# Second product of a two-layer token kernel: tasks of 256 columns with a shared fourth lane, another order of the work in the first steps and of the last stores

## The chip, the cores and the metric

The kernel runs on one core of one Trainium2 chip. The metric is the device time of one execution in microseconds, the median of ten runs. A core has a matrix engine (PE, with its weight loads shown apart as PEld), a vector engine (DVE), an activation engine (ACT), GpSimd (POOL), and a queue engine (SP) that here only issues transfers.

## The reference

`x` is 8 x 4096 x 192. Each of 8 heads (24 channels each) is convolved causally along the sequence with 7 taps, whose weights are a softmax of `weight`. The result, 32768 tokens of 192 channels, goes through two dense layers with a sigmoid gate between:

```python
w = np.exp(w); w = w / (np.sum(w, axis=-1, keepdims=True) + 1e-09)
out = np.einsum('hk,bskhg->bshg', w, x_unf)       # x_unf: 7 shifted copies of x
...
h = x @ w_in                                      # 192 -> 2048
g = h * (1.0 / (1.0 + np.exp(-1.702 * h)))
return (g @ w_out).astype(np.float32)             # 2048 -> 192
```

All of it is in 32-bit floats.

## The kernel before

**Steps.** The batch is split in two halves (n = 0, 1). A step takes 256 tokens of each half; there are 64 steps (`N_ST`), and two steps share one convolved chunk of 512 tokens (a "big"). A step has a first product (`w_in`), the gate, and a second product (`w_out`).

**Seven products instead of eight.** Both layers are seen as 2 x 2 block matrices times 2 x 2 block matrices (weights split by output half m and inner half, tokens by half n), and are multiplied with seven block products in a Strassen-Winograd scheme; step 0 alone uses the plain eight. For the second layer the seven are P1 = A11 B11, P2 = A12 B21, P3 = S4 B22, P4 = A22 T4, P5 = S1 T1, P6 = S2 T2, P7 = S3 T3. A and S are blocks of `w_out` and sums of them, B the gated activations, T sums of those (`sum_g`, on the vector engine).

**First product.** It is done in two units a and b of a step (half of the hidden channels each). `product1` issues four matmuls for each call, two on the upper and two on the lower 64 rows of the array, 256 columns each. A unit has the calls `p1`, `p2` (two), `p3` (two), `p4` (two), `p5`, `p5b`, `p6`, `p7`: eleven calls. Results go to PSUM tiles: three `slot` tiles that rotate (unit number modulo 3 gives `x`, the one before gives `z`), and one tile `sums`, which ACT fills with the first product of the unit (`seed`, a copy) and reads out twice (`keep2`, `keep3`). The vector engine adds `z` to the kept sums (`add22`, `add12`), ACT applies the gate (`h11`, `h21`, `h22`, `h12`).

**Second product.** `product2` gives one of the seven products: 96 output channels (three chunks of 32) by 256 tokens, summed over eight blocks j of 128 hidden channels. The array is used in four column lanes of 32. The table `LANES` cuts the 3 x 256 columns into four lanes of 192, so that for each j six matmuls are issued: lane 0 has 192 columns, lane 1 has 64 and 128, lane 2 has 128 and 64, lane 3 has 192. `output` issues P1, P3, P2 (added onto P1 in PSUM), P6, P7, P5, P4 into two banks each of the slots `ra` and `rb`, combines them on 128 partitions x 192 columns, transposes (`turn`), and `store` writes them out with 12 transfers on SP.

**What is hidden under PE.** The convolution of the next chunk runs on the vector engine. `prepare(big)` is a list of 31 pieces: 3 transposes of x, the load of the chunk after, a new buffer, 21 taps, 4 differences (`sums_c`) and `cross`, two transfers that copy the result to the other 64 partitions. `work(n)` runs the next n pieces at the place in the program where it stands. Each engine executes in the order of the program text; nothing reorders it (`manual_schedule`), and the waits between engines follow from the tiles that are read and written, a whole PSUM tile (both banks) at a time: a write of a slot waits for earlier reads of that slot.

**Names and lines of the profile:** L390 first-product matmul, L486 second-product matmul, L413 gate, L423 `seed`, L430 `keep2`, L443 `keep3`, L460 `add22`, L470 `add12`, L479 `sum_g`, L351/L353 taps, L360 `sums_c`, L336 transposes of x, L366 `cross`, L504 `turn`, L510/L514 copies of P1 and P3, L520 to L531 the combination, L543 stores, L665 the transposes of step 0.

Of the kernel before, what the change touches and what calls it, by code (L numbers as in the profile page):

```python
# [8 lines left out]
F32 = mybir.dt.float32  # L9
# [6 lines left out]
def kernel(  # L16
# [27 lines left out]
    nc = tc.nc  # L44
# [5 lines left out]
    P = 128  # L50
    R = 64
    Q = 32
    NC = D // R
    HF = F // 2
    HD = D // 2
    T = 256
    TA = 3 * T // 4
    TOK = 2 * T
    NF = F // P
    NK = NF // 2  # L60
# [11 lines left out]


    LANES = [
        (0, 0, 0, TA, 0),
        (1, 0, TA, T - TA, 0),
        (2, 1, T // 2, T // 2, 0),
        (3, 2, T - TA, TA, 0),
        (1, 1, 0, T // 2, T - TA),
        (2, 2, 0, T - TA, T // 2),  # L80
    ]
# [399 lines left out]
    def product2(slot, bank, a, b, first=True):  # L481
        dst = slot[:, bank, 0:TA]
        for j in range(NK):

            for l, c, t, n, at in LANES:
                nc.tensor.matmul(  # L486
                    dst[l * Q : (l + 1) * Q, at : at + n],
                    w_out_s[:, a, j, c * Q : (c + 1) * Q],
                    g[:, b, j, t : t + n],
                    start=(first and j == 0 and at == 0),  # L490
                    stop=(j == NK - 1),
                    skip_group_check=True,
                )
        return dst

    def output(s, last, work):

        ra, rb = last.x, last.z
        ut = u_pool.tile([P, 4, TA], F32, name="u")
        osb = osb_pool.tile([P, 2, TA // Q, 2 * Q], F32, name="osb")  # L500
        u1, u2, u3, u7 = (ut[:, i, :] for i in range(4))

        def turn(m, n, src):
            vec.transpose(  # L504
                osb[:, n, :, m * Q : (m + 1) * Q],
                src.rearrange("p (j t) -> p j t", t=Q),
            )

        p1 = product2(ra, 0, A11, B11)
        act.copy(u1, p1)  # L510
        for i in range(4):
            last.sum_g(i)
        p3 = product2(rb, 0, S4, B22)
        act.copy(u7, p3)  # L514
        work(2 if s > 1 else None)
        c11 = product2(ra, 0, A12, B21, first=False)
        turn(0, 0, c11)
        work(2)
        p6 = product2(rb, 1, S2, T2)
        vec.tensor_add(u2, u1, p6)  # L520
        work(3)
        p7 = product2(ra, 1, S3, T3)
        p5 = product2(ra, 0, S1, T1)
        vec.tensor_add(u3, u2, p7)  # L524
        vec.tensor_add(u1, u3, p5)
        vec.tensor_add(u2, u2, p5)
        turn(1, 1, u1)
        vec.tensor_add(u2, u2, u7)
        turn(0, 1, u2)
        p4 = product2(rb, 0, A22, T4)  # L530
        vec.tensor_sub(u3, u3, p4)  # L531
        turn(1, 0, u3)

        store(s, osb)

    def store(s, osb):
        big, odd = divmod(s, 2)
        p, c = divmod(big, CHUNKS)
        t = c * TOK + odd * T
        for n in (1, 0):  # L540
            rows = out_v[n, p, t : t + T, :].rearrange("(j i) (c e) -> c i j e", i=Q, e=2 * Q)
            for l, c, t0, nt, at in LANES:
                nc.sync.dma_start(  # L543
                    out=rows[c, :, t0 // Q : (t0 + nt) // Q, :],
                    in_=osb[l * Q : (l + 1) * Q, n, at // Q : (at + nt) // Q, :],
                )
# [3 lines left out]
    def work(n=None):  # L550
        for _ in range(len(todo) if n is None else min(n, len(todo))):
            todo.pop(0)()
# [22 lines left out]
    def first_step():  # L575
# [73 lines left out]
        osb = osb_pool.tile([P, 2, TA // Q, 2 * Q], F32, name="osb")  # L649
        for k in range(2):  # L650
            for n in range(2):
                for m in range(2):
                    src = product2(
                        slots[1 - n],
                        m,
                        (A11, A12, A21, A22)[2 * m + k],
                        (B11, B12, B21, B22)[2 * k + n],
                        first=(k == 0),
                    )
                    if k == 1:  # L660
                        if n == m == 0:
                            work(5)
                            sums_w_out()
                        work(1)
                        vec.transpose(  # L665
                            osb[:, n, :, m * Q : (m + 1) * Q],
                            src.rearrange("p (j t) -> p j t", t=Q),
                        )
        store(0, osb)
# [3 lines left out]
    for s in range(1, N_ST):  # L673
        a, b = nxt or Unit(s, 0), Unit(s, 1)
        if nxt is None:
            a.p1()
            a.seed()
            a.p5()
            a.p5b()
            a.p6()  # L680
        else:
            a.p6()
            a.p5()
            a.p5b()
        nxt = Unit(s + 1, 0) if s + 1 < N_ST and s != 1 else None
        a.keep2()
        a.p7()
        a.keep3()
        a.p2()
        a.h11()  # L690
        work(6)
# [4 lines left out]
        b.p1()  # L696
        b.seed()
        a.p3()
        work(None if s % 2 and s > 1 else 4)
# [12 lines left out]
        work(2)  # L712
# [13 lines left out]
        output(s, b, work)  # L726
        if s % 2 and (s + 3) // 2 < N_BIG:
            todo += prepare((s + 3) // 2)

# [29 lines left out]
```

## Time and profile before

| | us |
|---|---|
| median of 10 runs | 2478.3 (2476.86 to 2479.18) |
| the profiled execution, its own time | 2477.03 |
| its span, first to last instruction | 2475.2 |
| PE busy in the span | 2450.6 (99%) |
| vector engine busy | 1701.2 (69%) |
| ACT busy | 941.2 (38%) |
| mean granted TensorE clock | 0.997 |

The page gives for each engine its busy time, and for each source line the number of instructions, their busy time together, the mean of one and the idle time of the engine ahead of them. A matrix multiplication of 32-bit floats is executed as two passes, so the counts of matmuls in the profile are twice those of the program. Matmuls overlap each other, so a mean duration of one is not the time that it adds. From step 3 on the steps repeat: in the chain of waits the second product of a step takes 18.61 us and is followed by the next step's first product.

### The profile page before, as it was taken

The numbers are of one execution on the slowest core, as the hardware profiler recorded it, in microseconds if no ns is written. First come the engines' busy times: TensorE is split into PE (matmuls) and PEld (weight loads), VectorE is DVE, ScalarE is ACT, GpSimd is POOL, SyncE is SP. The second block draws the span as 40 slices with busy tenths as digits, with TensorE's granted clock in tenths as the row PEclk, the third lists the DMA queues.
The fourth block names the chain that finished last, engine by engine and source line by source line (L and its number), as shares of the span: only waits on it lengthen the run. The fifth ranks groups of instructions, "written<-read, shape, count | busy, mean of one in ns | idle before, by whom it ended". The sixth has DMA issues, their size and how long they took to land.

```text
span 2475.2 us, 114515 instructions
## 1 busy us (share of the span) xinstructions
PE 2450.6 (99%) x54434; PEld 2283.7 (92%) x54434; DVE 1701.2 (69%) x2348; ACT 941.2 (38%) x1052; POOL 8.1 (0%) x27
## 2 busy tenths in 40 slices
PE   8899999999999999999999999999999999999998
PEld 6899999999999999999999999999999999999998
DVE  8576666776666766667766667666677666676654
ACT  5243343343433433433434334334333343343342
POOL 1000000000000000000000000000000000000000
PEclk9999999999999999999999999999999999999999
DMA  7222221221221222212212212222122122122110
GB/s 180 46 55 47 45 58 39 48 57 38 55 59 30 57 47 45 58 38 47 58 38 54 59 29 57 47 45 57 41 46 58 38 54 59 29 58 44 24 35 16
DMA packets 197732, 123.58 MB, mean 50 GB/s; under 512 B 116048, under 2 KB 191440, under 8 KB 193296
## 3 DMA queue, kind: packets, MB, share of 16 engines
q1 hardware_dynamic: 196960, 115.48, 22.1%
q8 instruction: 425, 6.96, 1.2%
q0 software_dynamic: 288, 0.79, 0.1%
q14 instruction: 43, 0.35, 0.1%
q10 hardware_dynamic: 16, 0.00, 0.0%
HBM read 53.15 MB, written 25.17 MB: 32 GB/s over the span
## 4 chain that ended last, share of the span: by engine, by line
PE 97%; DVE 2%; DMA 0%; ACT 0%; issue 0%; SPq 0%; DVEq 0%; ACTq 0%
PE slot L486 48%; PE slot L390 31%; PE sums L390 18%; DVE g L479 0%; DVE f L353 0%; DMA f<-f 0%; DMA xin<-in_x_dram 0%; DVE xt L336 0%; ACT u L430 0%; ACT g L413 0%; SPq L114 0%; DVE u L460 0%; DVE f L360 0%; DVE w_out_s L249 0%; DVE f L244 0%
## 5 line engine op out<-in xcount | busy, mean ns | idle before, releaser
L486 PEld LDWEIGHTS slot<-g,w_out_s 128*32 128x32 f32 x43104 | 1192.2, 110 | 32.0 <-issue 24.0
L486 PE MATMUL slot<-g,w_out_s 128*32 128x128 f32 (+2 forms) x43104 | 1204.7, 274 | 9.1 <-DVE osb L665 5.0
L390 PE MATMUL slot<-f,w_in_s 64*128 64x256 f32 x7200 | 843.7, 376 | 0.6 <-DMA f<-f 0.5
L390 PEld LDWEIGHTS slot<-f,w_in_s 64*128 64x128 f32 x7200 | 693.0, 187 | 88.1 <-DVE u L460 1.4
L479 DVE TENSOR_TENSOR g<-g 128x1024 f32<-128x1024 f32 x504 | 600.1, 1222 | 192.4 <-ACT g L413 188.1
L390 PE MATMUL sums<-f,w_in_s 64*128 64x256 f32 x4080 | 512.0, 379 | 2.8 <-ACT u L430 2.3
L430 ACT COPY u<-sums 128x1024 f32<-128x1024 f32 x126 | 127.5, 1012 | 996.6 <-PE sums L390 996.6
L390 PEld LDWEIGHTS sums<-f,w_in_s 64*128 64x128 f32 x4080 | 390.6, 187 | 52.6 <-ACT u L430 3.1
L353 DVE SCALAR_TENSOR_TENSOR f<-xt,cw,f 128x512 f32<-128x512 f32 x564 | 421.8, 748 | 14.4
L413 ACT ACTIVATE g<-u 128x1024 f32<-128x1024 f32 x252 | 265.6, 1054 | 14.2 <-DVE u L470 14.1
L470 DVE TENSOR_TENSOR u<-u,slot 128x1024 f32<-128x1024 f32 x126 | 153.4, 1218 | 68.5 <-PE slot L390 68.5
L460 DVE TENSOR_TENSOR u<-u,slot 128x1024 f32<-128x1024 f32 x126 | 153.2, 1216 | 55.7 <-ACT u L443 55.7
L524 DVE TENSOR_TENSOR u<-u,slot 128x192 f32<-128x192 f32 x63 | 22.4, 355 | 244.5 <-PE slot L486 244.5
L443 ACT COPY u<-sums 128x1024 f32<-128x1024 f32 x126 | 127.5, 1012 | 130.8 <-PE sums L390 130.8
L413 ACT ACTIVATE g<-sums 128x1024 f32<-128x1024 f32 x128 | 130.5, 1019 | 94.7 <-PE sums L390 94.7
L413 ACT ACTIVATE g<-slot 128x1024 f32<-128x1024 f32 x132 | 135.5, 1027 | 50.1 <-PE slot L390 50.1
L423 ACT COPY sums<-slot 128x1024 f32<-128x1024 f32 x126 | 126.8, 1006 | 48.0 <-PE slot L390 46.0
L520 DVE TENSOR_TENSOR u<-u,slot 128x192 f32<-128x192 f32 x63 | 22.3, 354 | 92.0 <-PE slot L486 92.0
L514 ACT COPY u<-slot 128x192 f32<-128x192 f32 x63 | 20.1, 319 | 144.8 <-PE slot L486 144.8
L504 DVE STREAM_TRANSPOSE osb<-u 128x192 f32<-128x192 f32 x189 | 71.0, 376 | 4.3
L336 DVE STREAM_TRANSPOSE xt<-xin 128x576 f32<-128x576 f32 x96 | 67.1, 750 | 1.6 <-DMA xin<-in_x_dram 1.5
L360 DVE TENSOR_TENSOR f<-f 128x256 f32<-128x256 f32 x128 | 51.3, 422 | 2.2
(78 smaller groups left out, 287.5 us busy)
## 6 DMA issues: line engine op xcount, KB each, us to landing
xin<-in_x_dram SPq DMA_DIRECT2D x240, 180.0 KB, 4.3
f<-f SPq DMA_DIRECT2D x62, 576.0 KB, 4.8
out_dram<-osb SPq DMA_DIRECT2D x256, 48.0 KB, 1.7
out_dram<-osb SPq DMA_DIRECT2D x256, 32.0 KB, 1.6
out_dram<-osb SPq DMA_DIRECT2D x256, 16.0 KB, 1.5
g<-in_moe_w_in_dram SPq DMA_DIRECT2D x8, 384.0 KB, 9.3
g<-in_moe_w_out_dram SPq DMA_DIRECT2D x4, 768.0 KB, 5.5
xin<-in_x_dram SPq DMA_DIRECT2D x16, 160.0 KB, 3.1
```

Source lines behind the costliest of these rows:

```text
L336: vec.transpose(xts[big][:, c, :, :].rearrange("p n (j t) -> p (n j) t", t=Q), xins[big].rearrange("p n j d -> p (n j) d")[:, :, c * R : c ...
L353: vec.scalar_tensor_tensor(out=dst, in0=src, scalar=tap, in1=dst, op0=ALU.mult, op1=ALU.add)
L390: nc.tensor.matmul(slot[:, h, j * T : (j + 1) * T], w_in_s[halves[h], u, a, j * P : (j + 1) * P], f[halves[h], 0 if h == o else 1, b, :], ...
L413: act.activation(g[:, b, j : j + NK // NU, :].rearrange("p f t -> p (f t)"), src.rearrange("p h n -> p (h n)"), AF.Gelu_apprx_sigmoid,)
L423: act.copy(sums, self.x)
L430: act.copy(self.u2, sums)
L443: act.copy(self.u3, sums)
L460: vec.tensor_add(self.u3, self.u3, self.z)
L470: vec.tensor_add(self.u2, self.u2, self.z)
L479: vec.tensor_sub(v[dst], v[a], v[b])
L486: nc.tensor.matmul(dst[l * Q : (l + 1) * Q, at : at + n], w_out_s[:, a, j, c * Q : (c + 1) * Q], g[:, b, j, t : t + n], start=(first and j ...
L504: vec.transpose(osb[:, n, :, m * Q : (m + 1) * Q], src.rearrange("p (j t) -> p j t", t=Q),)
```

## The change

The second product is cut differently. A task (`product2`) now has 256 columns in each of the four lanes: lanes 0 to 2 are the three chunks of one product, and lane 3 is one chunk of P3 or P4. Five tasks carry P1, P2, P6, P5 and P7 in lanes 0 to 2; their fourth lanes carry the three chunks of P3 (with P1, P2, P6) and two of P4 (with P5, P7). The last chunk of P4 is made by `quarters`: each lane sums two of the eight j blocks, and the four quarters are added afterwards. P2 gets a place of its own in PSUM and is added on the vector engine. The results lie on 96 partitions x 256 columns, and chunks of P3 and P4 are copied by ACT to the partitions of their products. The stores are 6 transfers a step; in the last step two of the six go on ACT's queue.

Around it the order changes: in step 0 the quarters alternate between two slots and C22 is made in the fourth lanes; in the first product of every step P2 and P7 go ahead of P5; in steps 1 and 2 P1 of unit b is issued earlier, ahead of `keep3`; the pieces of the convolution are dealt otherwise, and the list for the next chunk is opened ahead of `output`, not after it.

```diff
     T = 256
-    TA = 3 * T // 4
     TOK = 2 * T
...
-    LANES = [
-        (0, 0, 0, TA, 0),
-        (1, 0, TA, T - TA, 0),
-        (2, 1, T // 2, T // 2, 0),
-        (3, 2, T - TA, TA, 0),
-        (1, 1, 0, T // 2, T - TA),
-        (2, 2, 0, T - TA, T // 2),
-    ]
...
-    def product2(slot, bank, a, b, first=True):
-        dst = slot[:, bank, 0:TA]
+    def product2(slot, bank, ab, last, first=True):
+
+        dst = slot[:, bank, 0:T]
+        tiles = [(c, *ab, c) for c in range(NC)] + [(NC, *last)]
         for j in range(NK):
-
-            for l, c, t, n, at in LANES:
+            for l, a, b, c in tiles:
                 nc.tensor.matmul(
-                    dst[l * Q : (l + 1) * Q, at : at + n],
+                    dst[l * Q : (l + 1) * Q, :],
                     w_out_s[:, a, j, c * Q : (c + 1) * Q],
-                    g[:, b, j, t : t + n],
-                    start=(first and j == 0 and at == 0),
+                    g[:, b, j, :],
+                    start=(first and j == 0),
                     stop=(j == NK - 1),
                     skip_group_check=True,
                 )
+        return dst[0 : NC * Q, :], dst[NC * Q :, :]
+
+    def quarters(slot, bank, a, b, c):
+
+        dst = [slot[l * Q : (l + 1) * Q, bank, 0:T] for l in range(4)]
+        for i in range(NK // 4):
+            for l in range(4):
+                j = NK // 4 * l + i
+                nc.tensor.matmul(
+                    dst[l],
+                    w_out_s[:, a, j, c * Q : (c + 1) * Q],
+                    g[:, b, j, :],
+                    start=(i == 0),
+                    stop=(i == NK // 4 - 1),
+                    skip_group_check=True,
+                )
         return dst
 
+    class Out:
+
+
+        def __init__(self, s):
+            self.s = s
+            self.osb = osb_pool.tile([NC * Q, 2, T // Q, 2 * Q], F32, name="osb")
+
+        def turn(self, m, n, src):
+            vec.transpose(
+                self.osb[:, n, :, m * Q : (m + 1) * Q],
+                src.rearrange("p (j t) -> p j t", t=Q),
+            )
+
+        def store(self):
+            big, odd = divmod(self.s, 2)
+            p, c = divmod(big, CHUNKS)
+            t = c * TOK + odd * T
+            for n in (1, 0):
+                rows = out_v[n, p, t : t + T, :].rearrange(
+                    "(j i) (c e) -> c i j e", i=Q, e=2 * Q
+                )
+                for c in range(NC):
+
+                    (act if c % 2 and self.s == N_ST - 1 else nc.sync).dma_start(
+                        out=rows[c], in_=self.osb[c * Q : (c + 1) * Q, n, :, :]
+                    )
+
+    def chunk(t, c):
+        return t[c * Q : (c + 1) * Q, :]
+
     def output(s, last, work):
 
         ra, rb = last.x, last.z
-        ut = u_pool.tile([P, 4, TA], F32, name="u")
-        osb = osb_pool.tile([P, 2, TA // Q, 2 * Q], F32, name="osb")
-        u1, u2, u3, u7 = (ut[:, i, :] for i in range(4))
-
-        def turn(m, n, src):
-            vec.transpose(
-                osb[:, n, :, m * Q : (m + 1) * Q],
-                src.rearrange("p (j t) -> p j t", t=Q),
-            )
-
-        p1 = product2(ra, 0, A11, B11)
+        out = Out(s)
+        u1, u2, p3, p4 = (
+            u_pool.tile([NC * Q, T], F32, name=f"u{i}") for i in range(4)
+        )
+
+        p1, p3c = product2(ra, 0, (A11, B11), (S4, B22, 0))
         act.copy(u1, p1)
+        act.copy(chunk(p3, 0), p3c)
         for i in range(4):
             last.sum_g(i)
-        p3 = product2(rb, 0, S4, B22)
-        act.copy(u7, p3)
-        work(2 if s > 1 else None)
-        c11 = product2(ra, 0, A12, B21, first=False)
-        turn(0, 0, c11)
+        p2, p3c = product2(rb, 0, (A12, B21), (S4, B22, 1))
+        act.copy(chunk(p3, 1), p3c)
         work(2)
-        p6 = product2(rb, 1, S2, T2)
+        vec.tensor_add(u2, u1, p2)
+        out.turn(0, 0, u2)
+        work(2)
+        p6, p3c = product2(ra, 1, (S2, T2), (S4, B22, 2))
+        act.copy(chunk(p3, 2), p3c)
         vec.tensor_add(u2, u1, p6)
         work(3)
-        p7 = product2(ra, 1, S3, T3)
-        p5 = product2(ra, 0, S1, T1)
-        vec.tensor_add(u3, u2, p7)
-        vec.tensor_add(u1, u3, p5)
-        vec.tensor_add(u2, u2, p5)
-        turn(1, 1, u1)
-        vec.tensor_add(u2, u2, u7)
-        turn(0, 1, u2)
-        p4 = product2(rb, 0, A22, T4)
-        vec.tensor_sub(u3, u3, p4)
-        turn(1, 0, u3)
-
-        store(s, osb)
-
-    def store(s, osb):
-        big, odd = divmod(s, 2)
-        p, c = divmod(big, CHUNKS)
-        t = c * TOK + odd * T
-        for n in (1, 0):
-            rows = out_v[n, p, t : t + T, :].rearrange("(j i) (c e) -> c i j e", i=Q, e=2 * Q)
-            for l, c, t0, nt, at in LANES:
-                nc.sync.dma_start(
-                    out=rows[c, :, t0 // Q : (t0 + nt) // Q, :],
-                    in_=osb[l * Q : (l + 1) * Q, n, at // Q : (at + nt) // Q, :],
-                )
+        p5, p4c = product2(rb, 1, (S1, T1), (A22, T4, 0))
+        q = quarters(rb, 0, A22, T4, 2)
+        act.copy(chunk(p4, 0), p4c)
+        vec.tensor_add(u1, u2, p5)
+        act.copy(chunk(p4, 2), q[2])
+        vec.tensor_add(p3, u1, p3)
+        out.turn(0, 1, p3)
+        for l in (0, 1, 3):
+            vec.tensor_add(chunk(p4, 2), chunk(p4, 2), q[l])
+        work(3)
+        p7, p4c = product2(ra, 0, (S3, T3), (A22, T4, 1))
+        act.copy(chunk(p4, 1), p4c)
+        vec.tensor_add(u1, u1, p7)
+        vec.tensor_add(u2, u2, p7)
+        out.turn(1, 1, u1)
+        vec.tensor_sub(u2, u2, p4)
+        out.turn(1, 0, u2)
+        out.store()
 
     todo = []
 
...
 
 
         todo.extend(prepare(1))
-        osb = osb_pool.tile([P, 2, TA // Q, 2 * Q], F32, name="osb")
+        out = Out(0)
+        c22 = u_pool.tile([NC * Q, T], F32, name="u0")
+        quarter = [(0, 0), (0, 1), (1, 0)]
         for k in range(2):
-            for n in range(2):
-                for m in range(2):
-                    src = product2(
-                        slots[1 - n],
-                        m,
-                        (A11, A12, A21, A22)[2 * m + k],
-                        (B11, B12, B21, B22)[2 * k + n],
-                        first=(k == 0),
-                    )
-                    if k == 1:
-                        if n == m == 0:
-                            work(5)
-                            sums_w_out()
-                        work(1)
-                        vec.transpose(
-                            osb[:, n, :, m * Q : (m + 1) * Q],
-                            src.rearrange("p (j t) -> p j t", t=Q),
-                        )
-        store(0, osb)
+            for i, (m, n) in enumerate(quarter):
+                c, c22c = product2(
+                    slots[i % 2],
+                    i // 2,
+                    ((A11, A12, A21, A22)[2 * m + k], (B11, B12, B21, B22)[2 * k + n]),
+                    ((A21, A22)[k], (B12, B22)[k], i),
+                    first=(k == 0),
+                )
+                if k == 1:
+                    work((6, 1, 3)[i])
+                    out.turn(m, n, c)
+                    act.copy(chunk(c22, i), c22c)
+                    if i == 0:
+                        sums_w_out()
+        out.turn(1, 1, c22)
+        out.store()
 
     first_step()
     nxt = None
...
             a.p5()
             a.p5b()
             a.p6()
+            a.keep2()
+            a.p2()
+            a.h11()
+            a.p7()
+            b.p1()
+            a.keep3()
         else:
             a.p6()
+            a.keep2()
+            a.p2()
+            a.h11()
+            a.p7()
+            a.keep3()
             a.p5()
             a.p5b()
         nxt = Unit(s + 1, 0) if s + 1 < N_ST and s != 1 else None
-        a.keep2()
-        a.p7()
-        a.keep3()
-        a.p2()
-        a.h11()
-        work(6)
+        work(4 if s > 1 else 9)
         a.add22()
         a.h22()
         a.p4()
         a.h21()
-        b.p1()
+        if s > 2:
+            b.p1()
         b.seed()
         a.p3()
-        work(None if s % 2 and s > 1 else 4)
+        work(None if s % 2 and s > 1 else 2)
         a.add12()
         b.p5()
         b.p6()
...
         if nxt:
             nxt.p1()
         b.p5b()
-        work(2)
+        work(1 if s > 1 else 2)
         a.sum_g(0)
         a.sum_g(1)
         b.add22()
...
         a.sum_g(3)
         b.add12()
         b.h12()
-        output(s, b, work)
+        if s == 1:
+            work(1)
         if s % 2 and (s + 3) // 2 < N_BIG:
             todo += prepare((s + 3) // 2)
+        output(s, b, work)
 
 
 # ---- launch: one core; inputs and outputs as the reference has them ----
```

## The prediction

> **What bounds the kernel now.** I read the page first. Its lines on the span, the engines, the chain of waits by engine, and the second product:
>
> ```profile
> span 2475.2 us, 114515 instructions
> PE 2450.6 (99%) x54434; PEld 2283.7 (92%) x54434; DVE 1701.2 (69%) x2348; ACT 941.2 (38%) x1052; POOL 8.1 (0%) x27
> PE 97%; DVE 2%; DMA 0%; ACT 0%; issue 0%; SPq 0%; DVEq 0%; ACTq 0%
> L486 PE MATMUL slot<-g,w_out_s 128*32 128x128 f32 (+2 forms) x43104 | 1204.7, 274 | 9.1 <-DVE osb L665 5.0
> ```
>
> PE is never out of work for long; half of its time is the line that the change rewrites. Freeing another engine brings nothing. There are two things to win: fewer nanoseconds per column in L486, and the few waits of PE. The chain of waits in a middle step (start, length, what) gives the size of one step, then P5/P5b and the later P6 of its first product:
>
> ```profile
> 1200.72 18.61 PE slot L486 x337
> 1220.40 1.73 PE slot L390 x16
> ...
> 1229.89 0.86 PE sums L390 x8
> ```
>
> The PE timeline of the start shows what doesn't repeat (start, length, last field the idle time ahead and its cause); the windows below it show the granted clock (the column after POOL):
>
> ```profile
> 44.66 13.40 PE L486 MATMUL slot<-g,w_out_s 128*32 128x192 f32 x480
> 62.55 7.96 PE L486 MATMUL slot<-g,w_out_s 128*32 128x192 f32 x192 [4.49 <-DVE osb L665]
> 71.00 2.84 PE L486 MATMUL slot<-g,w_out_s 128*32 128x192 f32 x96 [0.49 <-DVE osb L665]
> 73.77 2.86 PE L390 MATMUL slot<-f,w_in_s 64*128 64x256 f32 x24
> ...
> 95.27 10.76 PE L486 MATMUL slot<-g,w_out_s 128*32 128x192 f32 x384
> 108.32 7.07 PE L486 MATMUL slot<-g,w_out_s 128*32 128x192 f32 x185 [2.29 <-DVE osb L504]
> 117.10 3.12 PE L486 MATMUL slot<-g,w_out_s 128*32 128x128 f32 x103 [1.72 <-issue]
> 120.15 2.86 PE L390 MATMUL slot<-f,w_in_s 64*128 64x256 f32 x24
> ```
>
> ```profile
> 62.50:73.70 11.20, 10.66 (x288) 10.45 (x288) 2.66 (x5) 0.00 (x0) 0.00 (x0) 0.77 0.40 74
> 106.00:120.10 14.10, 10.09 (x290) 9.63 (x288) 4.31 (x13) 0.00 (x0) 0.00 (x0) 0.88 0.38 86
> ```
>
> The second product of step 0 takes 29.11 us (73.77 - 44.66) and that of step 1 24.88 (120.15 - 95.27); every later one takes 18.61. The 192 passes after the wait of 4.49 need 7.96, where two later tasks need 5.28: a wait costs itself and then slow clock.
>
> **What the Trainium skill says.** "TensorE: Matmul & The Clock Gate", section "Back-to-back issue gap", gives N/2.4 + 2.5 ns between matmuls of N columns: a fixed part for each instruction. The trace agrees. Sixteen passes of 256 columns on two row halves take 1.73 us, so 8 in a row, 215.8 ns each. In the second product, the copy of P1 starts at 1203.56 on ACT and the vector engine takes P4 at 1219.38; between lie six tasks, 15.82, so 2.64 each, or 329.6 ns for a j. A middle lane (64 and 128 columns, two passes each) has four passes and 384 columns in a j, a 256-column matmul two passes and 512. From 384a + 4b = 329.6 and 512a + 2b = 431.6, b is 2.4 ns. Section "What's actually happening" of that page says that the clock falls to half after an idle window of about 3.4 us; 0.77 and 0.88 above fit, though a wait of 2.29 was enough. "TensorEngine Tiling (Array Packing)", "Key Properties": a change of tiling mode drains the array. Seven tasks are 18.46, the stretch is 18.61: about 0.15 for the switch, which stays.
>
> **The change part by part.**
>
> Column work of a step: 7 x 3 chunks x 8 j x 256 columns on four lanes, before 7 x 8 x 192 and after 5 x 8 x 256 + 2 x 256, both 10,752 columns for each lane. Only the count of passes in the worst lane falls, from 7 x 8 x 4 = 224 to 42 x 2 = 84. After: 84 x 215.8 ns = 18.13, plus 0.15 for the switch. Against 18.61 that saves 0.33; with the 2.4 ns taken by itself, 140 x 2.4 = 0.34. In 62 steps (2 to 63): -21.1 us. The price is of row tiling, and the new lanes all begin together, which no row shows in column tiling. Bounds: nothing below (no fixed cost saved, 0) and 140 x 3.5 ns = 0.49 above, if the switch costs nothing. The loads (110 ns each, four side by side) lie under passes of 216 ns; today they lie under passes as short as 55 ns.
>
> Step 0: six tasks of 3.453 and 0.15 make 20.87, against 29.11: -8.2. The wait of 4.49 goes because the next task writes another slot than the one being transposed, and with it the slow clock. Next late would be the third task, at 62.1, which needs the transpose of slot 0 at 58.7 to 59.2 (ahead of `sums_w_out`): in time.
>
> Step 1: the seven taps and sums that stood ahead of the transposing of C11 (102.49 to 107.89) are dealt to four places, and the transpose of C11 no longer holds a slot. 24.88 to 18.28: -6.6. The first products of steps 1 and 2 take 21.5 each against 19.2 later, 0.86 of it an extra `p1`. In step 1 nine taps (about 6.6 us) now stand ahead of `add22`, which holds `p3`. In step 2 `p5` follows `p1` directly and must wait for the vector engine's reading of P7, about 1.4. The waits of 1.2 to 1.4 for `seed` go, others of that size come: +0.4 in all, from -2 to +3.
>
> Steady steps, waits of PE. Vector and ACT prices for 256 columns, from rows of 192 and 1024: an add 0.42 (0.355, 1.218), the next independent one 0.34 later, the next dependent one 0.46; a transpose 0.44 (0.376; 0.750 for 576), the next 0.36 later; an ACT copy 0.37 (0.32, 1.01); a tap 0.79 in a chain. ACT gets seven copies for two (+2.0 us a step), the vector engine ten adds and four transposes, about 6.0 for 3.6. Both have room, so only order counts. Take 0 at P1's start. P1 ends at 3.60, P2 at 7.06, P6 10.51, P5 13.96, the quarters 14.83, P7 18.28. `sum_g` is out of the way at 7.2, as now (its last ends at 1207.95, start 1200.65). Then two pieces, to 8.7, P2's add to 9.1: P5 needs it at 10.5. P6's add waits for ACT's copy out of the same slot: 11.05 to 11.5; P7 needs it at 14.8. P5's add waits for the quarters and an ACT copy: 15.4. P3's add, a transpose, three adds of quarters: 17.9. Three pieces, two adds of P7: slot free at 20.9 in odd steps, 20.4 in even ones. `p5` of the next step now stands after `p6`, `p2`, `p7`, at 18.28 + 0.2 + 4 x 0.863 = 21.9: in time. Two transposes and an add: 21.9. An even step then runs four taps (2.6), so `add22` goes from 24.6 to 25.8; `p3` comes at 26.2, in time. The chain behind it is what gets tight. Today in an odd step:
>
> ```profile
> 1224.37 1.21 DVE L460 TENSOR_TENSOR u<-u,slot 128x1024 f32<-128x1024 f32 x1
> 1225.68 1.05 ACT L413 ACTIVATE g<-u 128x1024 f32<-128x1024 f32 x1
> ...
> 1227.67 1.00 ACT L423 COPY sums<-slot 128x1024 f32<-128x1024 f32 x1
> ```
>
> From the end of `add22`, 1225.58, to the end of `seed`, 1228.67, are 3.1; P6 of unit b starts at 1229.89, 1.2 later. In the changed kernel `seed` ends at 28.8 to 28.9 in an even step, and P6 of b is ready at 18.28 + 0.2 + 12 x 0.863 = 28.84. So nothing is left: I take 0.1 for each of 30 even steps, +3. In odd steps the three differences and `cross` (1.3) are shorter than four taps, and 0.7 is left. Behind the waiting P6 stand all later matmuls, so a delay there is paid in full. `cross` now comes in the odd step right behind the stores on SP: six issues of 0.46, landing near 30; its reader, P1 of the next unit, comes at 32.3. In time.
>
> The end: today SP's issues run on and the last transfer lands 6.9 us after PE's end (2468.28).
>
> ```profile
> 2467.66 5.57 SPq L543 DMA_DIRECT2D out_dram<-osb  x12
> 2468.72 0.38 DVE L504 STREAM_TRANSPOSE osb<-u 128x192 f32<-128x192 f32 x1
> ```
>
> After: ACT copy, two adds, a subtract, two transposes, 2.5 for 0.8; but the first three issues start at 1.7, and SP has four of 0.46, to 3.55; 1.97 to landing as today: 5.5. -1.4.
>
> Sum: -21.1 - 8.2 - 6.6 + 0.4 + 3.0 - 1.4 = -33.9. On the profiled execution (2477.0) that is 2443.1; the median shown is 1.3 higher, so 2444.
>
> **The rivals.**
> A: the fixed part isn't saved, because four lanes that start and end together pay something instead (loads not quite covered). For it: today's lanes are staggered. Against: the row halves also run together and give 215.8. Then only start and end are won: 2478 - 13 = 2465.
> B: the vector chain is later than worked out by 0.3 to 0.8 us, and P6 of b waits for `seed`. For it: no slack; fourteen prices scaled from other sizes. At 0.5: 30 x 0.5 less the 3 taken is +12: 2456.
> C, the slower one: the same wait, so late that it loses more than all is worth. Each us d of delay costs 30 d in even steps and 31 (d - 0.7) in odd ones; with 36.9 to lose (33.9 and the 3 taken), it decides from d = 0.96 on. At 1.3: 39 + 19 against 36.9, so 2499. Against: it would need the fourteen prices to be off by 20% together.
> D: the start does not do what it is to do, one idle window stays (a load or `sums_w_out`): +7, 2451.
>
> **How the numbers follow.** Forecast 0.70 (2439 to 2450), D 0.07, B 0.10, A 0.06, C 0.07. The range takes in D, B and the lower costs of the forecast: 2438 to 2461; it leaves C, A and the far end of B out, about 0.17. A difference of 0.2% is about what a measurement can tell from none. Faster 0.91 (forecast, D, B, A), same 0.02, slower 0.07.
>
> **What would show it.** Right: 18.26 to 18.28 us from P1's start to the next first product in the chain of waits, half as many L486 instructions of one form, no wait of PE over 2 us before 130 us and a clock of 1.0 there. In even steps a wait of PE on `seed` of 0 to 0.3; vector engine near 1850 us busy. Wrong: a second product of 18.6 (A), a wait on `seed` of over 0.5 in each even step or any wait in odd ones (B, C), an idle stretch of PE over 2 us in step 0 or 1 (D).

## The result and the profile after

| | before | after |
|---|---|---|
| median, us | 2478.37 (2475.74 to 2481.02, 29 runs) | 2455.76 (2455.49 to 2458.59, 8 runs) |
| profiled execution, own time / span | 2477.03 / 2475.2 | 2457.4 / 2455.7 |
| instructions | 114,515 | 71,535 |

The ratio is 0.9911 (95%: 0.9902 to 0.9919): 22.6 us faster, where 34 were forecast. In the changed kernel L379 is the first-product matmul, L476 the second-product matmul, L492 the quarters, L412 `seed`, L449 `add22`, L342 a tap, L558 P5's add, L563 the adds of the quarters, L568 the second add of P7, L525 the stores. Its page (span, engines, chain by engine, the second product):

```profile
span 2455.7 us, 71535 instructions
PE 2435.2 (99%) x32882; PEld 1782.7 (73%) x32882; DVE 1838.1 (75%) x2600; ACT 1063.3 (43%) x1370; POOL 7.5 (0%) x27
PE 80%; DVE 13%; ACT 4%; issue 2%; DMA 1%; SPq 0%; DVEq 0%; ACTq 0%
L476 PE MATMUL slot<-g,w_out_s 128*32 128x256 f32 x20544 | 1133.3, 379 | 0.0
```

PE is busy 99% again, and that hides the story. The third line tells it: PE held 97% of the chain of waits and holds 80% now. For another 17% the chain runs through the vector engine and ACT: there PE had to wait for them. Yet the waits view of PE (what waited for what: us in total, times, longest) shows little:

```profile
PE sums L379 <- ACT sums L412: 5.2, 31, 0.2
...
PE slot L379 <- DVE u L568: 1.7, 1, 1.7
PE slot L379 <- DMA f<-f: 1.2, 2, 0.6
```

The second product is as forecast. In the chain of a middle step (start, length, what) its three pieces are 18.26 us, for 18.61:

```profile
1187.83 13.95 PE slot L476 x256
1201.78 0.86 PE slot L492 x16
1202.65 3.45 PE slot L476 x64
1206.10 1.06 PE sums L379 x8
```

In the PE timeline the starts of these stretches, with the idle time ahead and its cause in brackets, give steps 0 and 1 (44.92 to 65.78, and 87.20 to 105.47):

```profile
44.92 20.93 PE L476 MATMUL slot<-g,w_out_s 128*32 128x256 f32 x384
65.78 2.86 PE L379 MATMUL slot<-f,w_in_s 64*128 64x256 f32 x24
...
87.20 14.02 PE L476 MATMUL slot<-g,w_out_s 128*32 128x256 f32 x256
...
105.47 1.14 PE L379 MATMUL slot<-f,w_in_s 64*128 64x256 f32 x8
108.29 3.61 PE L379 MATMUL slot<-f,w_in_s 64*128 64x256 f32 x16 [1.69 <-DVE u L568]
...
163.58 1.77 PE L379 MATMUL slot<-f,w_in_s 64*128 64x256 f32 x13 [0.57 <-DMA f<-f]
```

The balance of the two profiled executions, from start to start of these stretches:

| place | forecast, us | measured, us |
|---|---|---|
| second products of steps 2 to 63, 62 x (18.611 to 18.267) | -21.1 | -21.3 |
| irregular longer second products of before, gone | - | -1.4 |
| second product of step 0 (29.11 to 20.86) | -8.2 | -8.3 |
| second product of step 1 (24.88 to 18.27) | -6.6 | -6.6 |
| first products of steps 1 and 2 (21.50, 21.50 to 21.42, 24.27) | +0.4 | +2.7 |
| first product of step 3 (19.19 to 20.96) | 0 | +1.8 |
| first products of the even steps from 4 on (19.20 to 19.70 in 29 of 30) | +3.0 | +14.8 |
| end | -1.4 | -1.2 |
| sum | -33.9 | -19.5 (spans: -19.6) |

The medians differ by 22.6, 3.0 more than the two profiled executions: that of before lies 1.3 under its median, that of after 1.6 above (a slow stretch of clock in step 2, run 4 below). All that was to be gained came. What is missing is the even steps, 11.8 us, and steps 1 to 3, 4.1. In the last even step, 62, no piece of the convolution is left to do, and it takes 19.19.

Where the even step loses 0.50 us is seen by holding it against the odd one ahead of it, in the PE timeline of the changed kernel:

```profile
1213.04 3.62 PE L379 MATMUL slot<-f,w_in_s 64*128 64x256 f32 x32
1216.49 1.03 PE L379 MATMUL sums<-f,w_in_s 64*128 64x256 f32 x8
1217.36 1.89 PE L379 MATMUL slot<-f,w_in_s 64*128 64x256 f32 x16
...
1250.50 3.68 PE L379 MATMUL slot<-f,w_in_s 64*128 64x256 f32 x32
1254.35 1.13 PE L379 MATMUL sums<-f,w_in_s 64*128 64x256 f32 x8 [0.17 <-ACT sums L412]
1255.32 1.89 PE L379 MATMUL slot<-f,w_in_s 64*128 64x256 f32 x16
```

P6 of unit b starts 3.45 after the group ahead of it in the odd step and 3.85 in the even one: 0.40 late. The next group follows after 0.87 and after 0.97: the restart costs 0.10. The view shows 0.17 of it as idle, because the modelled end of the last matmul (1250.50 + 3.68 = 1254.18) lies behind the time at which the next could have started (1250.50 + 3.45 = 1253.95). The chain of waits of the even step leads there (the second product began at 1225.2):

```profile
1240.57 0.43 DVE u L558
...
1242.85 0.42 DVE u L563
...
1243.29 0.76 DVE f L342
...
1250.05 1.22 DVE u L449
...
1253.30 1.00 ACT sums L412
```

P5's add, the last add of a quarter, three taps, `add22` (L449), the copy `seed` (L412): the queue that the prediction named.

### The profile page after: what moved, and what is told of

Its sections match the earlier page's. It is cut to its first block, busy times and chain, and to the rows that moved or that the text cites. A ratio compares the mean times of both kernels' runs of the same rounds, so it can differ in the third digit from the quotient of the medians.

```text
span 2455.7 us, 71535 instructions
## 1 busy us (share of the span) xinstructions
PE 2435.2 (99%) x32882; PEld 1782.7 (73%) x32882; DVE 1838.1 (75%) x2600; ACT 1063.3 (43%) x1370; POOL 7.5 (0%) x27
## 4 chain that ended last, share of the span: by engine, by line
PE 80%; DVE 13%; ACT 4%; issue 2%; DMA 1%; SPq 0%; DVEq 0%; ACTq 0%
PE slot L476 41%; PE slot L379 23%; PE sums L379 14%; DVE f L342 5%; PE slot L492 2%; ACT g L402 2%; DVE u L449 2%; DVE osb L510 2%; DVE u L563 2%; ACT sums L412 1%; DVE u L560 1%; DVE u L567 1%; DVE u L558 1%; DVE f L340 1%; ACT u L557 0%
## 5 line engine op out<-in xcount | busy, mean ns | idle before, releaser
L476 PE MATMUL slot<-g,w_out_s 128*32 128x256 f32 x20544 | 1133.3, 379 | 0.0
L476 PEld LDWEIGHTS slot<-g,w_out_s 128*32 128x32 f32 x20544 | 661.5, 110 | 450.7 <-issue 21.2
L379 PE MATMUL slot<-f,w_in_s 64*128 64x256 f32 x7200 | 848.6, 377 | 3.1 <-DVE u L568 1.7
L379 PEld LDWEIGHTS slot<-f,w_in_s 64*128 64x128 f32 x7200 | 692.3, 187 | 96.2 <-DVE u L449 7.6
L379 PE MATMUL sums<-f,w_in_s 64*128 64x256 f32 x4080 | 515.7, 381 | 6.3 <-ACT sums L412 5.2
L379 PEld LDWEIGHTS sums<-f,w_in_s 64*128 64x128 f32 x4080 | 388.6, 187 | 86.5 <-issue 25.1
L342 DVE SCALAR_TENSOR_TENSOR f<-xt,cw,f 128x512 f32<-128x512 f32 x564 | 421.6, 748 | 13.1
L449 DVE TENSOR_TENSOR u<-u,slot 128x1024 f32<-128x1024 f32 x126 | 153.2, 1216 | 39.6 <-PE slot L379 33.5
L558 DVE TENSOR_TENSOR u<-u,slot 96x256 f32<-96x256 f32 x63 | 26.3, 418 | 142.7 <-ACT u L557 142.7
L557 ACT COPY u<-slot 32x256 f32<-32x256 f32 x63 | 23.1, 367 | 249.0 <-PE slot L492 249.0
L412 ACT COPY sums<-slot 128x1024 f32<-128x1024 f32 x126 | 126.8, 1006 | 2.9 <-PE slot L379 0.7
L510 DVE STREAM_TRANSPOSE osb<-u 96x256 f32<-96x256 f32 x253 | 111.2, 439 | 6.9 <-ACT u L690 0.4
L552 ACT COPY u<-slot 32x256 f32<-32x256 f32 x63 | 23.0, 364 | 194.4 <-PE slot L476 194.4
L546 ACT COPY u<-slot 32x256 f32<-32x256 f32 x63 | 23.1, 367 | 170.5 <-PE slot L476 170.5
L566 ACT COPY u<-slot 32x256 f32<-32x256 f32 x63 | 23.1, 366 | 141.1 <-PE slot L476 141.1
```

The source lines that it names most:

```text
L342: vec.scalar_tensor_tensor(out=dst, in0=src, scalar=tap, in1=dst, op0=ALU.mult, op1=ALU.add)
L379: nc.tensor.matmul(slot[:, h, j * T : (j + 1) * T], w_in_s[halves[h], u, a, j * P : (j + 1) * P], f[halves[h], 0 if h == o else 1, b, :], ...
L412: act.copy(sums, self.x)
L449: vec.tensor_add(self.u3, self.u3, self.z)
L476: nc.tensor.matmul(dst[l * Q : (l + 1) * Q, :], w_out_s[:, a, j, c * Q : (c + 1) * Q], g[:, b, j, :], start=(first and j == 0), stop=(j == ...
L510: vec.transpose(self.osb[:, n, :, m * Q : (m + 1) * Q], src.rearrange("p (j t) -> p j t", t=Q),)
```

## The experiments

Runs 1 to 7 were taken on one chip and runs 8 to 11 on another. Beside them the kernel before took 2485 us (2485.3, 2484.8, 2484.8), not 2478; runs 10 and 11 deal with that. Times of the variants are compared with the changed kernel's 2455.8 (2456.5 in run 10), their steps by the traces. Runs 4, 9 and 11 are one execution each.

**1. One tap later.** In even steps from 4 on one tap moves from ahead of `add22` to behind P3.

```diff
-        work(4 if s > 1 else 9)
+        late = s > 2 and s % 2 == 0
+        work(3 if late else 4 if s > 1 else 9)
...
-        work(None if s % 2 and s > 1 else 2)
+        work(None if s % 2 and s > 1 else 3 if late else 2)
```

> Changed kernel, but in even steps from 4 on one tap of the convolution (0.79 us) moves from ahead of add22 to behind P3 of unit a. Theory (the late seed copy costs what the whole step shows, 0.50 us in 30 even steps: P6 of unit b starts 0.40 late and the matmuls restart 0.10 slower): every even step falls from 19.70 to 19.19 us in its first product, no wait of PE for the seed from step 4 on, 2455.8 - 15 = 2440.7 us. Rival (only the idle time that the waits view shows is lost, 0.17 us a time; the rest of the 0.50 is something else in even steps): -5, 2450.6 us, and even steps of 19.53. Rival (add12 now comes late behind three taps): a wait of P2 or of the gate in its place, 2455 us.

2441.84 us, 14 less; ratio to before on its chip 0.9829 (0.9815 to 0.9842). The first product of an even step is 19.195, as in odd ones. An even step in the timelines of PE and ACT of this run:

```profile
1168.29 3.62 PE L379 MATMUL slot<-f,w_in_s 64*128 64x256 f32 x32
1171.75 1.03 PE L379 MATMUL sums<-f,w_in_s 64*128 64x256 f32 x8
```

```profile
1170.31 1.00 ACT L412 COPY sums<-slot 128x1024 f32<-128x1024 f32 x1
```

`seed` now ends at 1171.31, 0.44 ahead of P6, and P6 follows after 3.46. So the whole 0.50 of a step hung on the late copy, of which the waits view shows 0.17; in 29 steps that is 14.6.

**2. One tap earlier.** The same with `work(5 ...)` ahead of `add22` and one tap behind P3.

> Changed kernel, but in even steps from 4 on one more tap (0.79 us) stands ahead of add22, one fewer behind it. Theory (the vector chain up to add22 sets the start of P6 of unit b in even steps, one for one; the restart is already paid): +0.79 in 30 steps, +23.7, 2479.5 us, first product of even steps 20.49. If P3 of unit a also waits for add22 and restarts: 0.1 more each, 2482.5. Rival (the wait is set by ACT's own order, not by the vector engine): no change, 2455.8.

2478.46 us, 22.7 more: the even steps are 20.48, +0.78. P3 waits as well:

```profile
1185.19 2.86 PE L379 MATMUL slot<-f,w_in_s 64*128 64x256 f32 x24 [0.58 <-DVE u L449]
1188.22 1.13 PE L379 MATMUL sums<-f,w_in_s 64*128 64x256 f32 x8 [0.17 <-ACT sums L412]
```

The vector chain sets the even step one for one. With one tap more, some 1.3 us for an even step in all, the time is that of the kernel before in its first runs (2478.4); beside the kernel before on its own chip (2485.3) a lead of 0.2% is left (ratio 0.9976, 0.9967 to 0.9986). So rival C of the prediction, a delay that eats the gain, was one tap away.

**3. Tasks in halves of 128 columns.** Twice the passes for the same columns and lanes.

```diff
+            for h in range(2):
+                cols = slice(h * T // 2, (h + 1) * T // 2)
                 for l, a, b, c in tiles:
...
-                    dst[l * Q : (l + 1) * Q, :],
+                        dst[l * Q : (l + 1) * Q, cols],
...
-                    g[:, b, j, :],
-                    start=(first and j == 0),
+                        g[:, b, j, cols],
+                        start=(first and j == 0 and h == 0),
```

> Changed kernel, but each 256-column matmul of the five tasks of a step is issued as two of 128 columns, same lanes and same columns: 80 more passes in a lane and step. Theory (the gain of the second product is the fixed 2.4 ns of a pass): +80 x 2.4 = 0.19 us in each of 63 steps and 0.2 in step 0, +12.3, of which the even steps give back up to 0.1 each because PE comes later to the late seed: 2465 to 2468 us, second product 18.46. Rival (the gain came from cutting lanes so that they start and end together, not from fewer passes): the second product stays at 18.27, 2455.8 us. Rival (twice the weight loads are no longer covered): over 18.6, above 2477 us.

The undisturbed second product is 18.468 us, 0.201 more: 80 passes at 2.5 ns, each with its weight load. The fixed price of a pass is shown. The time is 2477.4, 9 more than that explains. Of 61 second products (steps 2 to 62) 26 are longer than 18.47, by 14.6 us together, 12.5 of it in odd steps; step 0's takes 23.4 where 21.1 were due. The other 35 take 18.47, so loads that are no longer covered (the last rival) do not explain it. The even steps give back 0.27 each on average. PE waits for nothing that the profile shows (first the waits view, then PE and SP timelines of an odd step):

```profile
PE slot L478 <- issue: 7.9, 14, 1.4
```

```profile
338.99 3.03 PE L478 MATMUL slot<-g,w_out_s 128*32 128x128 f32 x100 [0.97 <-issue]
```

```profile
332.08 4.14 SPq L103 DMA_DIRECT2D xin<-in_x_dram  x8
```

The load of x was being issued from 332.1 to 336.2, and its last transfer landed at 341.9, past the stall. Of the 14 stalls 13 fall between the first issue of such a load and its landing; the loads together cover 12% of the span.

**4. Step 1's transposes behind P7's adds.** The three transposes of `work(3)` stand after the two adds of P7 in step 1.

```diff
-        work(3)
+        if s > 1:
+            work(3)
...
         vec.tensor_add(u2, u2, p7)
+        if s == 1:
+            work(3)
```

> Changed kernel, but in step 1 the three transposes of x (2.1 us on the vector engine) move from ahead of the two adds of P7 to behind them. Theory (step 2's P5 waits 1.69 us for those adds, and the wait slows the clock for some 3.4 us after it): no wait of PE on the add, clock 1.0 in step 2, its first product from 24.27 to about 21.5 us, 2.8 less in all. Rival (only the wait itself comes back; the slow clock is there for another reason): 1.7 less. Rival (add22 or the first taps come late in its place): nothing.

In steps 1 and 2 P5 still stands ahead of P2 and P7 (the order named under "The change" for every step begins with step 3), so in step 2 only P1 lies between the second product and P5. With the transposes moved the wait is 0.30 where it was 1.69, and step 2's first product 21.19 for 24.27. The time is 2454.35, 3.05 less than the profiled execution of the changed kernel (2457.4), though 1.4 less than its median. The difference lies in the clock of the execution: in runs 2, 9 and 10, whose step 2 is the same, the same wait of 1.69 is followed by full clock and its first product takes 22.58; in runs 1 and 5 it takes 24.26. The window from 105 to 130, first in the changed kernel's first profile, then in run 10 (the column after POOL is the clock):

```profile
105.00:130.00 25.00, 23.02 (x204) 19.76 (x200) 15.67 (x22) 13.05 (x15) 0.00 (x0) 0.93 0.41 83
```

```profile
105.00:130.00 25.00, 23.02 (x233) 19.31 (x228) 16.72 (x22) 14.66 (x16) 0.00 (x0) 1.00 0.41 82
```

So the move is worth 1.4 (22.58 to 21.19), and 1.7 more in executions in which the clock falls.

**5. P5 first again.** From step 3 on `p5` and `p5b` stand ahead of `p2` and `p7`, as in the kernel before.

```diff
             a.p6()
+            a.p5()
+            a.p5b()
             a.keep2()
-            a.p2()
-            a.h11()
             a.p7()
             a.keep3()
-            a.p5()
-            a.p5b()
+            a.p2()
+            a.h11()
```

> Changed kernel, but in the first product of steps from 3 on P5 stands ahead of P2 and P7 again, as before the change. Theory (P7 of the second product now comes last and its slot is free only some 1.1 to 2.4 us after it; P5 would wait for it, P2 and P7 cover that): P5 waits 1.2 us after even and 2.4 after odd steps and restarts, the late seed of even steps is then hidden: about +1.4 a step, 62 steps, 2540 us with full clock. Rival (the waits also slow the clock, as the single wait of 1.7 us in step 2 did): up to 1.7 more a step, 2640 us. Rival (the order is indifferent, ACT's copies would cover it): 2456 us.

2566.44 us, 110.7 more. The first products are 21.38 in even and 20.93 in odd steps, 1.7 more each; P5 waits for the second add of P7 in nearly every step (waits view, step 2's own wait counted in):

```profile
PE slot L379 <- DVE u L568: 100.4, 61, 1.9
```

The forecast of 1.4 was short at least in part because the same vector chain is late: in the changed kernel that add ends 20.7 us after the start of the second product in an even step and 21.2 in an odd one (1208.48 - 1187.76, 1246.40 - 1225.22), where the prediction had 20.4 and 20.9. Seven of the even steps take 23.07, 1.7 more than the others. In the first of them, step 4, the granted clock is 0.68 from 189 to 193 us, behind the wait; around the same wait of step 6 it is 1.00. So a wait here slows the clock in some steps, not in every one (mean clock 0.994). The new tasks need the new place of P2 and P7: without it they lose to the kernel before, at a ratio of 1.0329 (1.0312 to 1.0346).

**6. The kernel before with the new order of the start.** Its own tasks of 192 columns; step 0's quarters alternate between two slots, and pieces are dealt as in the changed kernel in step 1.

```diff
-                        slots[1 - n],
-                        m,
+                        slots[1 - m],
+                        n,
...
-        work(2 if s > 1 else None)
+        work(2)
...
-        work(6)
+        work(6 if s > 1 else 9)
```

> Kernel before (tasks of 192 columns, all of its second product), with the order of the start alone: step 0's quarters alternate between two slots, step 1 runs nine pieces ahead of add22 and two ahead of C11's transpose, not ten. Theory (the two waits in the second products of steps 0 and 1 and the slow clock behind them were 14 us of the time): step 0 from 29.1 to about 21.3, step 1 from 24.9 to 18.6, 2478.4 - 14 = 2464.4 us, if the later cross does not hold step 2. Rival (only the idle time comes back, the clock is slow anyway): -9, 2469 us. Rival (the work comes back as waits in the first products of steps 1 and 2): above 2472 us.

2472.11 us beside 2484.8 for the kernel before; ratio 0.995 (0.9938 to 0.9962), 12.7 less. Step 1's second product falls to 18.61, step 0's to 24.28, not to 21.3: a wait of 1.83 on step 0's transpose remains and one of 0.56 put down to issue.

```profile
62.80 5.06 PE L486 MATMUL slot<-g,w_out_s 128*32 128x192 f32 x171 [1.83 <-DVE osb L665]
```

The clock over the run is 1.0. So the start's order by itself is worth about 45% of the change (12.7 of the 28.3 by which the changed kernel leads the kernel before in run 10).

**7. All mended.** Runs 1 and 4 together, and six more pieces in step 2, so that the crossing transfer of step 3 isn't issued behind P3.

```diff
-        work(4 if s > 1 else 9)
+        late = s > 2 and s % 2 == 0
+        work(3 if late else {1: 9, 2: 6, 3: 5}.get(s, 4))
...
-        work(None if s % 2 and s > 1 else 2)
+        work(None if s % 2 and s > 1 else 2 if s == 1 else 3)
...
-        work(1 if s > 1 else 2)
+        work({1: 2, 2: 4}.get(s, 1))
```

> Changed kernel with three moves of pieces: the tap of even steps behind P3 (as the first run), step 1's transposes behind the adds of P7, and six more pieces of the convolution done in step 2 so that the crossing transfer of step 3 is issued early. Theory (what the changed kernel loses is the late seed in even steps, 15 us, step 2's wait with its slow clock, 2.8, and step 3's waits, 1.8): 2455.8 - 19.5 = 2436 us, first products of steps 3 and 4 at 19.2 to 19.7. Rival (the waits move to the next thing that is late, add12 or the gate): above 2445 us.

2438.34 us (2437.98 to 2438.43); ratio to before 0.981 (0.9797 to 0.9823). From step 3 on every first product but two is 19.20, every second product up to step 62 is 18.27. It is the fastest here, 17.4 below the changed kernel's first median. The even steps give 14.6 of that by the trace; step 2 takes 21.30 and step 3 19.20 for 20.96.

**8. Halves of 128 with the load elsewhere.** The load of x is issued with the first tap of its second chunk, in the first product of an even step.

```diff
-            yield lambda: load_x(big + 1)
+            yield lambda: None
...
-                yield lambda c=c, k=k: conv(big, c, k)
+                if (c, k) == (1, 0) and big + 1 < N_BIG:
+                    yield lambda c=c, k=k: (load_x(big + 1), conv(big, c, k))
+                else:
+                    yield lambda c=c, k=k: conv(big, c, k)
```

> The kernel with halves of 128 columns, but the load of the next chunk's x (8 transfers, 1.4 MB) is issued with the first tap of its second chunk, so in the first product of an even step and not in the second product of an odd one; number and place of all other pieces are unchanged. In that kernel PE stood for 7.9 us in 14 waits that nothing in the profile explains (issue), the long ones in second products of odd steps with this load under way. Theory (the instruction stream of PE, 6.8 MB in 417 packets, is held up by the load where matmuls are short): second products at 18.47 us in nearly all steps, the 14.6 us above that mostly gone, 2477.4 - 12 = 2465 us. Rival (the stream is too slow by itself at that rate): the waits stay, 2477 us. Rival (the load now holds up something in the first product or comes too late for the transposes): above 2477.

The waits put down to issue nearly vanish, and the excess of the second products falls from 14.6 to 4.2 us, in odd steps from 12.5 to 2.1:

```profile
PE slot L481 <- issue: 0.8, 2, 0.6
```

So a load under way is what stretches most of the odd second products; that it does so by holding up PE's instruction stream is argued, not shown. (The two runs are from two chips; the kernel before took the same time on both, 2485.3 and 2484.8.) The time fell only to 2473.19. The even first products take 19.65 on average again, for 19.44: in run 3, where PE came late out of an odd second product, it met a `seed` that was ready. So 6.3 of the 10.4 us were given back at the next wait.

**9. One queue for the last stores.** All six on SP.

```diff
-                    (act if c % 2 and self.s == N_ST - 1 else nc.sync).dma_start(
+                    nc.sync.dma_start(
```

> Changed kernel, but the last step's six stores are all on SP. Theory (an issue takes 0.46 us of its queue and the last lands some 2.4 us after the last issue ends): from the start of the last store's issue on SP to the end of the span 2 x 0.46 = 0.9 us more than now (4.2), so 5.1. Rival (the landing of the data sets the end, not the issues): 4.2 as now.

SP's part of the timeline here:

```profile
2449.72 2.84 SPq L525 DMA_DIRECT2D out_dram<-osb  x6
```

From there to the end of the span (2454.86) are 5.1; with two queues 4.2 (2451.50 to 2455.68). The second queue is worth 1.0 us.

**10 and 11. Both kernels once more, on one chip.**

> The changed kernel once more, for a chip on which the kernel before is slower than in its first runs (2485). Theory (the kernel before loses there in waits of its longer instruction stream, which the changed kernel hardly has): 2455.8 us as on the first chip, whatever the kernel before takes beside it. Rival (such a chip is slower for any kernel by 0.3%): 2462 us.

> The kernel before once more, for a profile beside the others of this call. Theory: its steps show 18.61 and 19.20 us as ever, and what it takes beyond 2478 is in second products with waits of PE put down to issue. Rival: its steps are longer evenly.

The changed kernel takes 2456.47 beside 2484.78 of the kernel before: ratio 0.9888 (0.9873 to 0.9903). It is the kernel before that is slower here. In its profile 23 second products of steps 2 to 62 are longer than 18.61, by 7.2 us together (1.4 in the first profile), step 1's takes 25.52 (24.88), and PE waits for nothing that the profile shows:

```profile
PE slot L486 <- issue: 4.0, 6, 2.4
```

In the changed kernel all 61 are 18.27, and PE has no such wait.

## Why the prediction was right, and what was mis-sized

The direction was right, and so were the mechanism and the size of the two large gains, the second product and the start. The size of the whole was not: 22.6 for 34. The time, 2455.8, lies in the stated range (2438 to 2461), but outside the 2439 to 2450 to which the forecast itself gave 0.70. It is in the range because that was drawn to take in rival B, which had 0.10, and in the even steps rival B is what happened.

- *Column work, -21.1.* Measured -21.3. The step from 224 to 84 passes, each with 2.4 ns, holds; run 3 puts 80 passes back and gets 0.201 us, 2.5 ns a pass. The fixed part of the Trainium skill's formula ("TensorE: Matmul & The Clock Gate", "Back-to-back issue gap": N/2.4 + 2.5 ns) thus shows in column tiling too, for lanes that start together. Its part for the columns does not fit this kernel: for 256 columns the formula gives, as an estimate, 109 ns, and the trace shows 215.8 for a pass; the two equations of the prediction give 0.834 ns a column, twice 1/2.4. So "the trace agrees" is right of the fixed part alone. Rival A fell.
- *Start, -8.2 and -6.6.* Measured -8.3 and -6.6; rival D fell. Run 6 shows it without the new tasks, but for 3 us in step 0.
- *"I take 0.1 for each of 30 even steps, +3".* This is the term that failed: 0.50 in each of 29 steps, 14.6, and 0.3 by which step 16 takes longer still (19.97; the kernel before has one such step too, the 41st, and the cause is open). The place and the queue were right. Three small errors lay in one margin: `seed` ended 29.1 after the start of the second product for 28.8 to 28.9; P6 could have started at 28.73 (1253.95 on the odd step's pattern, start 1225.22), not at 28.84; and the restart of PE, 0.10, was not counted at all. Of the first, 0.2 comes from places where I let one vector instruction overlap the next: the first tap after the quarters' adds came 0.44 behind the last of them (0.34 taken), P7's add 0.78 behind the last tap (0.67 in the row I read). Runs 1 and 2 show rival B's wait, one for one. That the measured time is also B's number, 2456, is partly luck: the 4.1 us of steps 1 to 3 are not in it, and they are made up for by the irregular stalls that went (1.4) and by the 3.0 between the medians and the profiled executions. The sign set for B, a wait on `seed` of over 0.5, did not show: the view had 0.17, inside the 0 to 0.3 that were to mean "right", while 0.50 were lost.
- *First products of steps 1 and 2, +0.4.* Measured +2.7; 1.7 of it was the slow clock behind the wait of step 2, which some executions show and others don't (run 4). So the clock of 1.0 ahead of 130 us, named as a sign, did not hold in the profiled execution (0.93 from 105 to 130). The wait for P7's adds, taken at about 1.4, was 1.69.
- *Cross "in time".* True from step 4 on. For step 3 it was worked out with the steady dealing of pieces, but only three pieces of the second chunk's list fit into step 1; its transfer was issued at 158.9, and step 3 waited 0.57 for it, besides a late `seed`: a wait in an odd step, which was to be a sign of being wrong. Run 7 removes both; they cost 1.8 us.
- *End, -1.4.* Measured -1.2, of which run 9 gives 1.0 to the second queue.
- *Not foreseen:* the irregularly longer second products of the kernel before are gone. They were worth 1.4 us in its first profile and 7.2 in that of run 11. They come back in run 3, where more and shorter matmuls do the same work; that the number of instructions is the cause is argued, not shown.

## What to carry to other kernels

Where a margin works out at zero, price a miss at its full cost: the lateness, not the idle time that the waits view shows, plus the restart of the pipeline; here 0.50 us for a visible 0.17, in every second step. Then look for one piece of work on the late queue that can stand behind the wait: one tap moved gave back 14 us. A cut of matmuls into fewer, longer ones is worth its fixed cost per pass, and here stalls of PE that no semaphore explains went with it.

## What the hardware showed that I had not expected

- A wait of PE of 1.69 us in step 2 was followed by half clock in three profiles (granted clock 0.50 from 109 to 111.9 us in the changed kernel's first, where the 16 passes behind the wait took 3.61 us; so too in runs 1 and 5) and by full clock in three others with the same program there (runs 2, 9 and 10; 2.00 us in run 10). In run 5 seven of the even steps, whose waits were 1.92 us, took 1.7 us longer; of the odd ones, with waits of 1.47, none did.
- With matmuls of 128 columns an x load under way went with stalls of PE of up to 1.4 us that no semaphore explains; with the load elsewhere 7.9 us of them fell to 0.8.
- An issue of a store took 0.46 us of SP's time (four in 1.83); the two on ACT's queue took 0.39 and 0.32, the second behind the last transpose.
